# A convolution-and-MLP kernel on one core: halving the first chunk, doubling weights on ScalarE, softmax one chunk ahead, and the last addition by an accumulating DMA

## The chip, the cores and the metric

One core of a Trainium2 chip. The metric is the time on the device in microseconds (us), median of several executions. The kernel before took 477.84 us when it was first timed (477.68 to 479.58, 3 runs). All profiles used here are of undisturbed ("fast") executions; the profiler's span is some 1.5 us shorter than the time (476.3 against 477.84). "Clock" is the clock that TensorE was granted, as a share of its full one.

## The reference

For every position a softmax over 7 taps in each of 8 heads gives weights for a causal convolution of x. Its output goes through a layer that is the larger of two products, and through an output product.

```python
B, S, D, H, K = 8, 4160, 192, 8, 7           # F = 1024
w = np.exp(weight_gen - weight_gen.max(-1, keepdims=True))
w = w / (w.sum(-1, keepdims=True) + 1e-9)     # softmax over the K taps
x_pad = concat([zeros(B, K-1, D), x], axis=1)
y[b,s,h,:] = sum_k w[b,s,h,k] * x_pad[b, s+k, h,:]       # 24 values per head
g = np.maximum(y @ w1, y @ w2)                # 33280 x 1024
out = g @ w_out                               # 33280 x 192
```

## The kernel before

Each of 128 partitions holds 260 consecutive positions ("columns"). They are cut into chunks: three of 8 columns (0, 1, 2), fourteen of 16 (3 to 16), and two of 8 and 4. TensorE works in units of 8 columns (chunk 0 is two units of 4). The maximum is computed as y·w1 + relu(y·(w2−w1)); wd is w2−w1, and w10E, w10O, w10R are w1·w_out, computed on the chip at the start.

In these traces engines run their own instructions in program order, and so do the queues from which SyncE (SP) and GpSimd (POOL) issue DMAs: what the program writes earlier stands ahead.

```python
def conv(ci):                                   # VectorE, one chunk
    ...
    nc.vector.reduce_sum(out=sum_t, in_=...)    # e_t is exp(weight_gen), by ScalarE
    nc.vector.reciprocal(out=rec_t, in_=sum_t)
    nc.vector.tensor_tensor(                    # softmax product, each weight written twice
        out=_sub(en_t, 0, [[2, TH], [2 * TH, K], [1, 2]]),
        in0=_sub(e_t, 0, [[K, TH], [1, K], [0, 2]]),
        in1=_sub(rec_t, 0, [[1, TH], [0, K], [0, 2]]), op=ALU.mult)
    nc.vector.tensor_tensor(out=m_t, ...)       # weights times x, all taps ("product")
    if ci + 2 < len(CHUNKS):
        load(ci + 2)                            # POOL: wg_t and xb_t
    ... three additions: 7 taps to 1, the last into y_t
...
def transpose(u):                               # SP: y_t transposed into yt
    nc.sync.dma_start_transpose(out=yt..., in_=y_ts[ci]...)
def evac(u, i):                                 # ScalarE: 384 columns of TensorE's output to o_t
    nc.scalar.copy(...)
    ... after the last: nc.sync.dma_start(out=out..., in_=o_t)
...
for u in range(NU + 1):
    while queued < NCH and queued <= UNITS[min(u + 3, NU - 1)][0]:
        exp(queued); conv(queued); queued += 1
    if u == 0: transpose(0)
    if u + 1 < NU: transpose(u + 1)
    for i in range(4):                          # quarters of a unit on TensorE
        hid_main(u, 2 * i); hid_rest(u, 2 * i); relu(u, 2 * i) ...
        evac of the pair of columns before; output matmuls of unit u - 1; second hid, relu
```

The softmax here doesn't subtract the row's maximum and nothing guards it: scores larger than these inputs give would overflow.

## Time and profile before

| quantity | before | view it is read from |
|---|---|---|
| time | 477.84 us | times |
| span | 476.3 us | page |
| VectorE, one 16-column chunk | 25.61 us | timeline, from product to product |
| TensorE, one chunk at full clock | 25.24 us | timeline, eight quarters of 3.155 us |
| first hidden matmul / first of chunk 3 | 31.4 / 88.41 us | timeline |
| from chunk 3 to the end | 387.9 us | 476.3 − 88.41 |

The slices of the page (the span in 40 parts of 11.9 us; a digit is the busy share in tenths) for TensorE, VectorE and the granted clock:

```profile
PE   0087695599999999999999999989999999999997
DVE  2949999999999999999999999999999999997000
PEclk9999698599999999999999999999999999999999
```

From the ninth slice on (after 95 us), TensorE is full but for one slice at 8 and the end, and its clock is at 9 tenths or over.

In the group rows that follow, and in the prediction, a row gives line, engine, operation, output<-inputs, their shapes and the count, then busy us in all and mean ns of one, then idle us before them and what ended it. PE is TensorE, DVE VectorE, ACT ScalarE; PEld is the loading of weights, SPq SP's queue.

### The profile page before, as it was taken

The page shows a single profiled execution, that of the slowest core. Times are in us where ns is not written, and L with a number is a line of the kernel's source. Part 1 is how long each engine was busy: PE and PEld are TensorE (multiplying, and loading weights), DVE is VectorE, ACT ScalarE, POOL GpSimd, SP SyncE. Part 2 cuts the span into 40 slices and gives each one's busy share as a digit, 9 for nine tenths or more (in the row PEclk, how much of TensorE's full clock was granted, in tenths as well). Part 3 has the DMA queues.
Part 4 walks back from the last instruction along what each step waited for, and adds up shares of the span by engine and source line. Part 5 has one row for each costly group of instructions (what it writes and reads, how often), then busy time and mean ns, then how long its engine had stood idle before and what let it go on. Part 6 is the DMA issues. An engine that isn't in the chain of part 4 may idle for free.

```text
span 476.3 us, 8155 instructions
## 1 busy us (share of the span) xinstructions
PE 427.1 (90%) x3606; PEld 271.5 (57%) x3606; DVE 418.6 (88%) x136; ACT 336.5 (71%) x437; POOL 22.1 (5%) x46
## 2 busy tenths in 40 slices
PE   0087695599999999999999999989999999999997
PEld 0054353366666666666666666656666666666675
DVE  2949999999999999999999999999999999997000
ACT  1266374287877878787878787867878787777773
POOL 3000000000000000000000000000000000000000
PEclk9999698599999999999999999999999999999999
DMA  8945745546574737467585747384736537273212
GB/s 168 261 107 104 170 120 129 133 93 169 131 175 123 199 107 174 150 139 190 131 200 125 206 85 219 76 192 109 200 109 139 172 67 200 43 200 100 83 67 100
DMA packets 62131, 67.47 MB, mean 142 GB/s; under 512 B 52329, under 2 KB 53609, under 8 KB 60304
## 3 DMA queue, kind: packets, MB, share of 16 engines
q1 hardware_dynamic: 57792, 41.12, 31.1%
q0 software_dynamic: 4304, 25.84, 24.9%
q8 instruction: 28, 0.46, 0.4%
q14 instruction: 7, 0.06, 0.0%
HBM read 46.58 MB, written 25.56 MB: 151 GB/s over the span
## 4 chain that ended last, share of the span: by engine, by line
PE 81%; DVE 11%; DMA 5%; SPq 1%; ACT 1%; issue 0%; POOLq 0%
PE op_ps L292 34%; PE hdp L243 22%; PE hdp L258 13%; PE op_ps L279 7%; DVE m_t L138 5%; PE op_ps L287 4%; DMA wso<-in_moe_w_out_dram 3%; DVE m_t L149 2%; DMA yt<-y_t 2%; DVE m_t L151 1%; DVE en_t L130 1%; PE pw L211 1%; DVE y_t L154 1%; DMA wg_t<-in_weight_gen_dram 1%; DVE sum_t L125 1%; DVE rec_t L127 1%
## 5 line engine op out<-in xcount | busy, mean ns | idle before, releaser
L269 ACT ACTIVATE rd_t<-hdp 128x1024 bf16<-128x1024 f32 (+1 forms) x272 | 267.5, 986 | 112.0 <-PE hdp L258 77.2
L292 PE MATMUL op_ps<-wo,rd_t 128*128 128x192 bf16 x2080 | 216.6, 248 | 0.0
L292 PEld LDWEIGHTS <-rd_t 128*128 128x128 bf16 x2080 | 177.8, 99 | 23.7 <-issue 0.9
L138 DVE TENSOR_TENSOR m_t<-xb_t,en_t 128x21504 bf16<-128x21504 bf16 (+2 forms) x19 | 185.0, 9738 | 5.5 <-DMA xb_t<-zero_t 4.9
L243 PE MATMUL hdp<-yt,wdE 128*128 128x512 bf16 (+1 forms) x272 | 101.6, 374 | 20.8 <-DMA yt<-y_t 18.3
L243 PE MATMUL hdp<-yt,wdO 128*128 128x512 bf16 (+1 forms) x272 | 101.5, 373 | 0.0
L258 PE MATMUL hdp<-yt,wdR 64*128 64x512 bf16 (+1 forms) x544 | 81.6, 375 | 1.1 <-ACT rd_t L269 1.1
L149 DVE TENSOR_TENSOR m_t<-m_t 128x9216 bf16<-128x9216 bf16 (+2 forms) x19 | 81.0, 4263 | 0.7
L303 ACT COPY o_t<-op_ps 128x384 f32<-128x384 f32 x130 | 61.6, 474 | 2.5 <-PE op_ps L292 2.3
L151 DVE TENSOR_TENSOR m_t<-m_t 128x6144 bf16<-128x6144 bf16 (+2 forms) x19 | 55.0, 2894 | 0.7
L258 PEld LDWEIGHTS <-wdR 64*128 64x128 bf16 x544 | 16.2, 94 | 58.1 <-issue 57.5
L279 PE MATMUL op_ps<-w10R,yt 128*128 128x384 bf16 x130 | 44.0, 339 | 0.0
L279 PEld LDWEIGHTS <-yt 128*128 128x128 bf16 x130 | 12.4, 96 | 53.1 <-issue 52.8
L243 PEld LDWEIGHTS <-wdE 128*128 128x128 bf16 x272 | 26.8, 99 | 22.0 <-DMA yt<-y_t 19.6
L287 PEld LDWEIGHTS <-yt 128*128 128x128 bf16 x260 | 25.7, 99 | 14.8 <-issue 0.6
L130 DVE TENSOR_TENSOR en_t<-e_t,rec_t 128x1792 bf16<-128x1792 bf16 (+2 forms) x19 | 33.4, 1755 | 0.7
L287 PE MATMUL op_ps<-w10E,yt 128*128 128x192 bf16 x130 | 32.2, 248 | 0.0
L287 PE MATMUL op_ps<-w10O,yt 128*128 128x192 bf16 x130 | 32.2, 248 | 0.0
L154 DVE TENSOR_TENSOR y_t<-m_t 128x3072 bf16<-128x3072 bf16 (+2 forms) x19 | 29.0, 1527 | 0.7
L243 PEld LDWEIGHTS <-wdO 128*128 128x128 bf16 x272 | 26.8, 99 | 3.6 <-issue 3.4
L125 DVE TENSOR_REDUCE sum_t<-e_t 128x128 f32<-128x896 bf16 (+2 forms) x19 | 17.9, 944 | 9.9 <-ACT e_t L115 9.9
L105 POOL DMA_DIRECT2D xb_t<-in_x_dram x18 | 9.5, 529 | 333.4 <-DVE m_t L138 333.4
(29 smaller groups left out, 69.0 us busy)
## 6 DMA issues: line engine op xcount, KB each, us to landing
out_dram<-o_t SPq DMA_DIRECT2D x31, 768.0 KB, 3.9
xb_t<-in_x_dram POOLq DMA_DIRECT2D x14, 1056.0 KB, 7.8
wg_t<-in_weight_gen_dram POOLq DMA_DIRECT2D x14, 448.0 KB, 6.1
xb_t<-in_x_dram POOLq DMA_DIRECT2D x3, 672.0 KB, 7.9
wg_t<-in_weight_gen_dram POOLq DMA_DIRECT2D x4, 224.0 KB, 5.5
wso<-in_moe_w_out_dram SPq DMA_DIRECT2D x1, 768.0 KB, 13.5
out_dram<-o_t SPq DMA_DIRECT2D x2, 384.0 KB, 3.6
yt<-y_t SPq DMA_TRANSPOSE x34, 3.8
```

The source lines that it names most:

```text
L130: nc.vector.tensor_tensor(out=_sub(en_t, 0, [[2, TH], [2 * TH, K], [1, 2]]), in0=_sub(e_t, 0, [[K, TH], [1, K], [0, 2]]), in1=_sub(rec_t, ...
L138: nc.vector.tensor_tensor(out=m_t, in0=_sub(xb_t, 0, [[D, K], [1, n]]), in1=_sub(en_t, 0, [[2 * TH, K], [2, TH], [0, D // H // 2], [1, 2]] ...
L149: nc.vector.tensor_tensor(out=m_t[:, 0:3 * n], in0=m_t[:, 0:3 * n], in1=m_t[:, 3 * n:6 * n], op=ALU.add)
L151: nc.vector.tensor_tensor(out=rows(m_t, 2, 2, 0), in0=rows(m_t, 2, 2, 0), in1=rows(m_t, 5, 2, 1), op=ALU.add)
L154: nc.vector.tensor_tensor(out=y_t, in0=m_t[:, 0:n], in1=m_t[:, 2 * n:3 * n], op=ALU.add)
L243: nc.tensor.matmul(hd_ts[u, f][:, j * 512:j * 512 + N], lhsT=wd[kind][:, f * P:(f + 1) * P], rhs=_sub(yt_ts[u], 2 * j * P, [[3 * P, n // 2 ...
L258: nc.tensor.matmul(hd_ts[u, f][:, j * 512:j * 512 + N], lhsT=wd["R"][r, f * P:(f + 1) * P], rhs=_sub(yt_ts[u][r, :], P, [[3 * P, n // 2], ...
L269: nc.scalar.activation(out=_sub(rd_ts[u], f * 1024, [[512, 2], [1, N]]), in_=_sub(hd_ts.pop((u, f)), 0, [[512, 2], [1, N]]), func=AF.Relu,)
L279: nc.tensor.matmul(op[:, 0:2 * D], lhsT=yt[:, (3 * i + 1) * P:(3 * i + 2) * P], rhs=w10R, start=True, stop=False, skip_group_check=True,)
L287: nc.tensor.matmul(op[:, sl], lhsT=yt[:, (3 * i + 2 * j) * P:(3 * i + 2 * j + 1) * P], rhs=(w10E, w10O)[j], start=False, stop=False, skip_ ...
L292: nc.tensor.matmul(op[:, sl], lhsT=rd[:, f, j * 512 + i * P:j * 512 + (i + 1) * P], rhs=wo[:, f * D:(f + 1) * D], start=False, stop=(f == ...
L303: nc.scalar.copy(out=o_ts[u][:, 2 * i * D:2 * (i + 1) * D], in_=op_ts.pop((u, i))[:, 0:2 * D])
```

## The change

The intent is to take work off VectorE, the slower of two balanced engines, and to start earlier. The first chunk is computed in two halves, and its halo (the six positions ahead of it) is masked by a bitwise AND in place of a DMA of zeros. From chunk 2 on the softmax product writes each weight once, and ScalarE doubles it (dup). The softmax runs a chunk ahead. The last addition becomes an accumulating DMA. The weights' subtraction moves to GpSimd, and two evacuations become one of 768 columns. The transposes move to the end of the unit before. The functions are soft (the softmax), mul (the product), adds (the additions) and dup.

```diff
+            halo = xb_t[:, 0:PAD * D].bitcast(I32)
+            nc.vector.tensor_scalar(out=halo, in0=halo, scalar1=msk[:, 0:1], scalar2=None,
+                                    op0=ALU.bitwise_and)
...
-            out=_sub(en_t, 0, [[2, TH], [2 * TH, K], [1, 2]]),
+                out=_sub(en_t, 0, [[pair, N], [pair * N, K], [1, pair]]),   # pair is 1 from chunk 2
...
+    def dup(ci):
+        nc.scalar.copy(out=_sub(en_t, 0, [[2, KTH], [1, 2]]),
+                       in_=_sub(e1_ts.pop(ci), 0, [[1, KTH], [0, 2]]))
...
+            nc.vector.tensor_tensor(out=z_t, in0=m_t[:, 0:n], in1=m_t[:, n:2 * n], op=ALU.add)
+            nc.vector.tensor_tensor(out=y, in0=m_t[:, 2 * n:3 * n], in1=m_t[:, 6 * n:7 * n], op=ALU.add)
+            nc.gpsimd.dma_start(out=y, in_=z_t, accum_op=ALU.add, max_dma_last_dim=4096)
...
-            nc.vector.tensor_tensor(out=dst, in0=ws[kind, 1], in1=ws[kind, 0], op=ALU.subtract)
+            nc.gpsimd.tensor_tensor(out=dst, in0=ws[kind, 1], in1=ws[kind, 0], op=ALU.subtract)
+        soft(1)
+        mul(1)
+        load(3)
...
         nc.gpsimd.memset(w10R, 0.0)            # unchanged, but load(3) now stands ahead of it
...
-        if u + 1 < NU:
-            transpose(u + 1)
         for i in range(4):
...
+            if ca is not None:                 # u is the last unit of chunk ca - 1
+                if i == 1:
+                    dup(ca + 1); adds(ca); mul(ca + 1); load(ca + 3)
+                if i == 2:
+                    exp(ca + 2); soft(ca + 2)
+            if i == 3 and u + 1 < NU:
+                transpose(u + 1)
```

(The conditions for the last chunks left out.)

More of the change, by code (lines that the diff above doesn't have):

```diff
@@ L11 @@
 BF16 = mybir.dt.bfloat16
+I32 = mybir.dt.int32
 AF = mybir.ActivationFunctionType
@@ L41 @@
     FCH = F // P
+    DIRECT = 2
     CPP = B * S // P
@@ L76 @@
     wg_ts, xb_ts, y_ts, yt_ts = {}, {}, {}, {}
-    e_ts = {}
-    zero_t = consts.tile([P, PAD * D], BF16, name="zero_t")
-    nc.vector.memset(zero_t, 0.0)
+    e_ts, e1_ts, en_ts, m_ts = {}, {}, {}, {}
+    msk = consts.tile([P, 1], I32, name="msk")
+    nc.gpsimd.iota(msk, pattern=[[0, 1]], base=0, channel_multiplier=1)
+    nc.vector.tensor_single_scalar(out=msk, in_=msk, scalar=RPB - 1, op=ALU.bitwise_and)
+    nc.vector.tensor_scalar(out=msk, in0=msk, scalar1=1, scalar2=-1, op0=ALU.min, op1=ALU.mult)
     def load(ci):
@@ L84, in load @@
         wg_t = pwg.tile([P, To * WGC], FP32, name="wg_t", tag="wg")
-        nc.gpsimd.dma_start(
+        (nc.sync if ci == 0 else nc.gpsimd).dma_start(
             out=wg_t,
@@ L92, in load @@
         if c0 == 0:
+            nc.gpsimd.memset(xb_t[0:1, 0:PAD * D], 0.0)
             nc.gpsimd.dma_start(
@@ L102, in load @@
             )
-            nc.sync.dma_start(out=xb_t[0:P:RPB, 0:PAD * D], in_=zero_t[0:P:RPB, :])
+            halo = xb_t[:, 0:PAD * D].bitcast(I32)
+            nc.vector.tensor_scalar(out=halo, in0=halo, scalar1=msk[:, 0:1], scalar2=None,
+                                    op0=ALU.bitwise_and)
         else:
@@ L116, in exp, with pieces, soft @@
         e_ts[ci] = e_t
-    def conv(ci):
-        To = sum(CHUNKS[ci][1])
-        n = To * D
-        TH = To * H
+    def pieces(ci):
+        return [(0, 4), (4, 4)] if ci == 0 else [(0, sum(CHUNKS[ci][1]))]
+    def soft(ci):
+        TH = sum(CHUNKS[ci][1]) * H
         e_t = e_ts.pop(ci)
@@ L127, in conv @@
         nc.vector.reciprocal(out=rec_t, in_=sum_t)
-        en_t = pen.tile([P, K * TH * 2], BF16, name="en_t", tag="en")
+        pair = 2 if ci < DIRECT else 1
+        for o, To in pieces(ci):
+            N = To * H
+            if pair == 2:
+                en_t = pen.tile([P, K * N * 2], BF16, name="en_t", tag=f"en{o}")
+                en_ts[ci, o] = en_t
+            else:
+                en_t = pe_.tile([P, K * N], BF16, name="e1_t", tag="e1")
+                e1_ts[ci] = en_t
+            nc.vector.tensor_tensor(
+                out=_sub(en_t, 0, [[pair, N], [pair * N, K], [1, pair]]),
+                in0=_sub(e_t, o * WGC, [[K, N], [1, K], [0, pair]]),
+                in1=_sub(rec_t, o * H, [[1, N], [0, K], [0, pair]]),
+                op=ALU.mult,
+            )
@@ new lines, in dup, with mul @@
+    def dup(ci):
+        if ci not in e1_ts:
+            return
+        KTH = K * sum(CHUNKS[ci][1]) * H
+        en_t = pen.tile([P, KTH * 2], BF16, name="en_t", tag="en0")
+        nc.scalar.copy(out=_sub(en_t, 0, [[2, KTH], [1, 2]]),
+                       in_=_sub(e1_ts.pop(ci), 0, [[1, KTH], [0, 2]]))
+        en_ts[ci, 0] = en_t
+    def mul(ci, o=0):
+        To = dict(pieces(ci))[o]
+        n = To * D
+        m_t = pm.tile([P, K * n], BF16, name="m_t", tag="m")
+        m_ts[ci, o] = m_t
@@ L130, in conv @@
         nc.vector.tensor_tensor(
-            out=_sub(en_t, 0, [[2, TH], [2 * TH, K], [1, 2]]),
-            in0=_sub(e_t, 0, [[K, TH], [1, K], [0, 2]]),
-            in1=_sub(rec_t, 0, [[1, TH], [0, K], [0, 2]]),
+            out=m_t,
+            in0=_sub(xb_ts[ci], o * D, [[D, K], [1, n]]),
+            in1=_sub(en_ts[ci, o], 0, [[2, K * To * H], [0, D // H // 2], [1, 2]]),
             op=ALU.mult,
         )
-        xb_t = xb_ts.pop(ci)
-        m_t = pm.tile([P, K * n], BF16, name="m_t", tag="m")
@@ L138, in conv, with adds, rows @@
-        nc.vector.tensor_tensor(
-            out=m_t,
-            in0=_sub(xb_t, 0, [[D, K], [1, n]]),
-            in1=_sub(en_t, 0, [[2 * TH, K], [2, TH], [0, D // H // 2], [1, 2]]),
-            op=ALU.mult,
-        )
-        if ci + 2 < len(CHUNKS):
-            load(ci + 2)
-        def rows(t, step, cnt, at):
-            return _sub(t, at * n, [[step * n, cnt], [1, n]])
+    def adds(ci, o=0):
+        T_all = sum(CHUNKS[ci][1])
+        n = dict(pieces(ci))[o] * D
+        m_t = m_ts.pop((ci, o))
+        def rows(at, step, cnt):
+            return _sub(m_t, at * n, [[step * n, cnt], [1, n]])
@@ L149, in conv @@
         nc.vector.tensor_tensor(out=m_t[:, 0:3 * n], in0=m_t[:, 0:3 * n],
                                 in1=m_t[:, 3 * n:6 * n], op=ALU.add)
-        nc.vector.tensor_tensor(out=rows(m_t, 2, 2, 0), in0=rows(m_t, 2, 2, 0),
-                                in1=rows(m_t, 5, 2, 1), op=ALU.add)
-        y_t = py.tile([P, n], BF16, name="y_t", tag="y")
-        nc.vector.tensor_tensor(out=y_t, in0=m_t[:, 0:n], in1=m_t[:, 2 * n:3 * n], op=ALU.add)
-        y_ts[ci] = y_t
+        if o == 0:
+            y_ts[ci] = py.tile([P, T_all * D], BF16, name="y_t", tag="y")
@@ new lines, in adds @@
+        y = y_ts[ci][:, o * D:o * D + n]
+        if ci < DIRECT:
+            nc.vector.tensor_tensor(out=rows(0, 2, 2), in0=rows(0, 2, 2), in1=rows(1, 5, 2),
+                                    op=ALU.add)
+            nc.vector.tensor_tensor(out=y, in0=m_t[:, 0:n], in1=m_t[:, 2 * n:3 * n], op=ALU.add)
+        else:
+            z_t = py.tile([P, n], BF16, name="z_t", tag="z")
+            nc.vector.tensor_tensor(out=z_t, in0=m_t[:, 0:n], in1=m_t[:, n:2 * n], op=ALU.add)
+            nc.vector.tensor_tensor(out=y, in0=m_t[:, 2 * n:3 * n], in1=m_t[:, 6 * n:7 * n],
+                                    op=ALU.add)
+            nc.gpsimd.dma_start(out=y, in_=z_t, accum_op=ALU.add, max_dma_last_dim=4096)
@@ L159 @@
     load(0)
+    exp(0)
+    soft(0)
     ident = consts.tile([P, P], BF16, name="ident")
@@ L183 @@
         )
-        exp(0)
-        conv(0)
+        exp(1)
+        for o in (0, 4):
+            mul(0, o)
+            adds(0, o)
+        load(2)
         for kind, dst in (("E", wd["E"]), ("T", wd["R"][0:64, :])):
-            nc.vector.tensor_tensor(out=dst, in0=ws[kind, 1], in1=ws[kind, 0], op=ALU.subtract)
+            nc.gpsimd.tensor_tensor(out=dst, in0=ws[kind, 1], in1=ws[kind, 0], op=ALU.subtract)
+        soft(1)
+        mul(1)
+        load(3)
         nc.sync.dma_start(out=wd["R"][64:P, :], in_=wd["E"][0:64, :])
@@ L276, in out_first @@
         yt = yt_ts[u]
-        op = pps_o.tile([P, 512], FP32, name="op_ps", tag="op")
-        op_ts[u, i] = op
+        if i % 2 == 0:
+            op_ts[u, i // 2] = pps_o.tile([P, 1024], FP32, name="op_ps", tag="op")
+        op = op_ts[u, i // 2][:, i % 2 * 512:i % 2 * 512 + 2 * D]
         nc.tensor.matmul(
-            op[:, 0:2 * D], lhsT=yt[:, (3 * i + 1) * P:(3 * i + 2) * P], rhs=w10R,
+            op, lhsT=yt[:, (3 * i + 1) * P:(3 * i + 2) * P], rhs=w10R,
             start=True, stop=False, skip_group_check=True,
@@ L284, in out_col @@
     def out_col(u, i, j):
-        yt, rd, op = yt_ts[u], rd_ts[u], op_ts[u, i]
-        sl = slice(j * D, (j + 1) * D)
+        yt, rd, op = yt_ts[u], rd_ts[u], op_ts[u, i // 2]
+        sl = slice(i % 2 * 512 + j * D, i % 2 * 512 + (j + 1) * D)
         nc.tensor.matmul(
@@ L297, in out_col, with evac @@
             )
-    def evac(u, i):
+    def evac(u, g):
         ci, o, n = UNITS[u]
-        if i == 0:
+        if g == 0:
             o_ts[u] = pout.tile([P, n * D], FP32, name="o_t", tag="o")
-        nc.scalar.copy(out=o_ts[u][:, 2 * i * D:2 * (i + 1) * D],
-                       in_=op_ts.pop((u, i))[:, 0:2 * D])
-        last = u == NU - 1
-        if i == n // 2 - 1 or last:
-            a = 2 * i if last else 0
-            b = 2 * i + 2
+        nc.scalar.copy(out=_sub(o_ts[u], 4 * g * D, [[2 * D, 2], [1, 2 * D]]),
+                       in_=_sub(op_ts.pop((u, g)), 0, [[512, 2], [1, 2 * D]]))
+        if g == n // 4 - 1:
             nc.sync.dma_start(
-                out=bass.AP(tensor=out.tensor, offset=(CHUNKS[ci][0] + o + a) * D,
-                            ap=[[CPP * D, P], [1, (b - a) * D]]),
-                in_=o_ts[u][:, a * D:b * D],
+                out=bass.AP(tensor=out.tensor, offset=(CHUNKS[ci][0] + o) * D,
+                            ap=[[CPP * D, P], [1, n * D]]),
+                in_=o_ts[u],
             )
     NCH = len(CHUNKS)
-    queued = 1
+    exp(2)
+    soft(2)
+    transpose(0)
     prev_evac = None
     for u in range(NU + 1):
-        while queued < NCH and queued <= UNITS[min(u + 3, NU - 1)][0]:
-            exp(queued)
-            conv(queued)
-            queued += 1
-        if u == 0:
-            transpose(0)
-        if u + 1 < NU:
-            transpose(u + 1)
+        ends_chunk = u < NU - 1 and UNITS[u + 1][0] != UNITS[u][0]
+        ca = UNITS[u][0] + 1 if ends_chunk else None
         for i in range(4):
@@ L349 @@
                 out_col(u - 1, q, 1)
-                prev_evac = (u - 1, q)
+                if q % 2 == 1:
+                    prev_evac = (u - 1, q // 2)
+            if ca is not None:
+                if i == 1:
+                    if ca + 1 < NCH:
+                        dup(ca + 1)
+                    adds(ca)
+                    if ca + 1 < NCH:
+                        mul(ca + 1)
+                    if ca + 3 < NCH:
+                        load(ca + 3)
+                if i == 2 and ca + 2 < NCH:
+                    exp(ca + 2)
+                    soft(ca + 2)
+            if i == 3 and u + 1 < NU:
+                transpose(u + 1)
     if prev_evac is not None:
```

## The prediction

> **What bounds the kernel now.** I read the page's header and slices first, then the groups by line and shape, then busy time by stretch, then the timeline in order of time at the places where TensorE stands still. The group rows that carry the steady state:
>
> ```profile
> PE 427.1 (90%) x3606; PEld 271.5 (57%) x3606; DVE 418.6 (88%) x136; ACT 336.5 (71%) x437; POOL 22.1 (5%) x46
> ...
> L138 DVE TENSOR_TENSOR m_t<-xb_t,en_t 128x21504 bf16<-128x21504 bf16 x14 | 159.0, 11359 | 0.5
> L149 DVE TENSOR_TENSOR m_t<-m_t 128x9216 bf16<-128x9216 bf16 x14 | 69.4, 4958 | 0.5
> L303 ACT COPY o_t<-op_ps 128x384 f32<-128x384 f32 x130 | 61.6, 474 | 2.5 <-PE op_ps L292 2.3
> L151 DVE TENSOR_TENSOR m_t<-m_t 128x6144 bf16<-128x6144 bf16 x14 | 47.0, 3357 | 0.5
> L130 DVE TENSOR_TENSOR en_t<-e_t,rec_t 128x1792 bf16<-128x1792 bf16 x14 | 28.4, 2025 | 0.5
> L154 DVE TENSOR_TENSOR y_t<-m_t 128x3072 bf16<-128x3072 bf16 x14 | 24.6, 1758 | 0.5
> L125 DVE TENSOR_REDUCE sum_t<-e_t 128x128 f32<-128x896 bf16 x14 | 15.1, 1078 | 0.0
> L127 DVE RECIPROCAL rec_t<-sum_t 128x128 f32<-128x128 f32 x14 | 13.3, 953 | 0.5
> ```
>
> There are 14 full chunks of 16 columns. VectorE's seven rows sum to 11.36+4.96+3.36+2.03+1.76+1.08+0.95 = 25.5 us; in the timeline its products start 25.61 us apart. TensorE repeats a quarter of an 8-column unit every 3.155 us, so a chunk costs it 8 x 3.155 = 25.24 us. The two engines are balanced to 1.5%, VectorE being the slower. Busy time by stretch shows where this balance is not yet reached:
>
> ```profile
> 40.00:50.00 10.00, 4.31 (x41) 2.63 (x37) 9.79 (x8) 4.02 (x8) 1.07 (x2) 0.83 0.87 187
> 80.00:90.00 10.00, 1.59 (x6) 0.27 (x6) 9.86 (x6) 0.00 (x0) 0.00 (x0) 0.54 0.68 155
> 200.00:300.00 100.00, 100.00 (x859) 63.69 (x856) 99.17 (x29) 79.70 (x100) 4.28 (x8) 1.00 0.63 157
> ```
>
> (Columns: stretch, length, busy PE, PEld, DVE, ACT, POOL, then granted clock, DMA share, GB/s.) Until 90 us TensorE starves while VectorE is full; afterwards both are full. The timeline ties them:
>
> ```profile
> 82.76 1.76 DVE L154 TENSOR_TENSOR y_t<-m_t 128x3072 bf16<-128x3072 bf16 x1
> ...
> 313.28 1.76 DVE L154 TENSOR_TENSOR y_t<-m_t 128x3072 bf16<-128x3072 bf16 x1
> ...
> 320.38 0.39 PE L243 MATMUL hdp<-yt,wdE 128*128 128x512 bf16 x1 [1.76 <-DMA yt<-y_t]
> ```
>
> Chunk 3 (counting from 0), the first full one, leaves VectorE at 84.5, its transpose lands, and TensorE resumes at 88.41 (3.9 us later). At 320 TensorE has used up its lead and waits again. So **the end is set by "when does y leave VectorE, plus its way to TensorE"**, not by busy shares.
>
> [...] the 1056 KB x load, which reads twice that in fp32, took 7.8 us to land, [...] exp over 448 and 896 elements took 570 and 943 ns, slope 0.833. [...]
>
> **The change part by part.**
>
> *VectorE, full chunk.* The weights are no longer written twice: 896 instead of 1792 elements, 1.09 us (the measured 128x896 form) for 2.03, saves 0.93. The adds of 3.36+1.76 become two of 3072 elements, 2 x 1.76, saves 1.6. VectorE needs 25.5-2.5 = 23.0 us. It stops being the bound.
>
> *ScalarE, full chunk.* The doubling copy of 1792 elements costs 0.19+0.833 x 1792 = 1.69 us. Two 384-column evacuations of 0.474 become one 768-column one, about 0.8 by the slope, four times: saves 0.6. Its load goes from 20.1 us (measured in 25.24) to about 21.2, still under 25.24. But ScalarE works in program order, and the doubling, an evacuation and the exp fall within one and a half quarters of a unit. From the steady timeline: relu of an odd tile ends 3.63 us after its quarter begins and its buffer is needed again at 3.95, a slack of 0.3. After the doubling, the fifth tile's relu waits for relu, 1.59 doubling, 0.92 relu, 0.70 evacuation (durations less about 0.1 overlap) and ends 4.66 into the next quarter instead of 3.63, 0.7 past need. So **TensorE loses about 0.7 us per chunk**, 25.24 to 25.9.
>
> *The new loop.* The order of instructions shows: in the last unit of chunk c, VectorE does adds(c+1), product(c+2), softmax(c+3); product(c+2) needs the doubling, which ScalarE does only after the fourth relu of that unit. With c starting on TensorE at 0: last unit at 12.6; fourth relu starts 5.8 later, 0.9, doubling 1.7: 21.1. Product 11.4, softmax of the next chunk 3.1, adds 8.5: y(c+2) leaves VectorE at 44.1. Then the accumulating DMA, new on the path: [...] 5.6 us, call it an estimate. Then the transpose 3.9. **Chunk c+2 can start at 53.7, where TensorE wants it at 2 x 25.24 = 50.5 (51.9 with the doubling's stalls).**
>
> *Start.* The zero-row DMA goes (VectorE waited 4.9 us for it), and the weight loads start some 5 us earlier. But x and weights then share the DMA rates, so I start the first product at 12 as before, at best 9.5. The subtraction on GpSimd stands behind the load of chunk 2, which waits for the second half's product: about 21 us, done by 25 to 27, hence first matmul near 31 as before. VectorE's work to y(3): 11.7 (two halves) +2.3+5.8+1.8+5.3+5.8+3.1+4.5+11.4+3.1+8.5 = 63.2 us (the 1.8 being softmax(2)), plus 1.7 waiting for the doubling of chunk 2: 77. Plus 5.6+3.9: TensorE starts chunk 3 at 86, against 88.4. The missing idle of 6.6 us (waiting for an exp at 32 us) is mostly paid back by the DMA add.
>
> *Sum.* Chunk 3 at 86; chunk 4 at 86+25.9 = 111.9; then two chunks per 53.7: chunk 16 at 111.9+6 x 53.7 = 434.1. From chunk 16's start (421.35) to the span's end was 55.0 before; with the stall 55.7. Span 489.8, plus 1.5 between span and time: **491 us**.
>
> **Rivals.**
> A. *The DMA add is quick (below 4 us).* For: DMA is idle then, since the x load was issued when the product ended. Then TensorE bounds with doubling stalls: 86+13 x 25.9+55.7+1.5 = 480.
> B. *Neither costs anything*, the intended outcome: 86+13 x 25.24+55+1.5 = 470.6, 1.5% faster. More than 2% needs chunk 3 to start below 83.7 and no loss later: possible only if x lands at 9.5.
> C. *Long stalls cool the clock.* Before, stalls of 6 to 10 us were followed by matmuls at half speed; the 1.76 us stall at 320 was not. My stalls are 2 to 3 us. If they cool it, about 1.7 us is added at each of six: 501. The same end follows if the add takes 7.5 us.
> D. *GpSimd's subtraction and VectorE block each other* at 21 to 28 us: up to 4 us later at the start, largely hidden.
>
> **Range and chances.** Main line 491, A 480, B 471, C 501. Weighted mostly on main line and A I say 489, range 474 to 502. The 2% lines are 468.3 and 487.4: faster 0.09, within 0.33, slower 0.58.
>
> **What would show it.** The DMA add's issue to landing near 5.6 us; TensorE waiting on the transpose about 3 us at every second chunk, the chain of waits running through product, adds, DMA add and transpose; VectorE idle before products, waiting for the doubling copy, and busy 23.0 per chunk; short waits of TensorE for relu after each doubling; chunk 3 starting near 86. I am wrong if the add takes under 4 us, if the doubling runs earlier than 21 us into the chunk, or if the first y comes much before 20 us.

## More of the kernel before

SP's own waits (what ended the wait: total us, times, longest):

```profile
SPq L227 <- DVE y_t L154: 271.5, 17, 19.1
```

SP mostly stands ready at a transpose and waits for y_t, so a transpose is issued as soon as VectorE is done. How long the transposes then take, from the view of the tile yt:

```profile
DMA to landing us min/median/max: 2.9/3.8/5.5
```

None takes over 5.5 us; this is to be held against the same line of later kernels.

## The result

The changed kernel takes 553.64 us (median, 552.77 to 554.76, 4 runs) against 477.76 for the kernel before in the same rounds. The ratio is 1.158, with a 95% interval of 1.154 to 1.162: **slower by 15.8%**. Ratios here are the mean time of one kernel's runs over that of the other's of the same rounds, all of them fast but for two of x1's, so they are not quite the ratio of the medians. The direction was predicted; the size, 489 in a range of 474 to 502, was not.

The page of the changed kernel: busy times, then slices of TensorE and of the clock.

```profile
PE 445.6 (81%) x3606; PEld 277.7 (50%) x3606; DVE 424.7 (77%) x141; ACT 351.8 (64%) x389; POOL 49.1 (9%) x66
...
PE   0518756399969999699959997799959995999996
...
PEclk9959779599998999799988999799979999899999
```

TensorE has the same 3606 matmuls but 18.5 us more busy time, and every fourth or fifth slice is a hole in PE and in its clock. VectorE, meant to be relieved, is busy 424.7 us instead of 418.6. The groups by shape and the DMA issues (KB each, median us from issue to landing) say why:

```profile
L147 DVE TENSOR_TENSOR e_t<-e_t,rec_t 128x896 bf16<-128x896 bf16 x14 | 58.1, 4151 | 0.5
...
L160 ACT COPY en_t<-e_t 128x1792 bf16<-128x1792 bf16 x14 | 23.5, 1678 | 0.5 <-DVE e_t L147 0.5
```

```profile
y_t<-z_t POOLq DMA_DIRECT2D x14, 768.0 KB, 7.2
```

The softmax product, half the elements, takes 4.15 us where it took 2.03. The doubling copy costs 1.68 us, as predicted (1.69). The DMA add takes 7.2 us. The waits (total, times, longest):

```profile
DVE m_t L170 <- ACT en_t L160: 80.7, 16, 13.0
...
PE hdp L295 <- DMA yt<-y_t: 60.3, 10, 12.6
...
PE hdp L295 <- ACT w10R L268: 11.9, 1, 11.9
```

VectorE stands before its products for 80.7 us in all, waiting for the doubling (the longest, 13.0, before the last chunk of 4 columns). TensorE waits 60.3 us for transposes and 11.9 us for w10R. One round of the loop, from the timeline (start, duration, engine, line, operation; in brackets the idle time before and what ended it):

```profile
166.62 0.61 PE L295 MATMUL hdp<-yt,wdE 128*128 128x512 bf16 x1 [5.92 <-DMA yt<-y_t]
...
187.30 1.68 ACT L160 COPY en_t<-e_t 128x1792 bf16<-128x1792 bf16 x1
...
189.01 11.36 DVE L170 TENSOR_TENSOR m_t<-xb_t,en_t 128x21504 bf16<-128x21504 bf16 x1 [7.67 <-ACT en_t L160]
...
202.38 4.14 DVE L147 TENSOR_TENSOR e_t<-e_t,rec_t 128x896 bf16<-128x896 bf16 x1
...
213.02 1.75 DVE L197 TENSOR_TENSOR y_t<-m_t 128x3072 bf16<-128x3072 bf16 x1
...
215.08 1.23 POOL L199 DMA_DIRECT2D y_t<-z_t  x1 [13.87 <-DVE y_t L197]
...
222.37 1.42 SPq L279 DMA_TRANSPOSE yt<-y_t  x1
...
226.06 0.61 PE L295 MATMUL hdp<-yt,wdE 128*128 128x512 bf16 x1 [5.92 <-DMA yt<-y_t]
```

This is a closed chain: the doubling stands behind ScalarE's fourth relu, which waits for TensorE; it lets VectorE multiply, and two steps later TensorE gets its input, two chunks further on. It takes 59.4 us here, and 60.3 on average over six rounds ((467.67 − 105.86)/6, the starts of chunks 3 and 15), where TensorE's work needs 50.5.

The start, in the timelines of GpSimd (its subtractions, load(3) and the memset), VectorE (the second half's last two additions) and TensorE (the first hidden matmul):

```profile
23.37 2.76 POOL L236 TENSOR_TENSOR wdE<-ws1E,ws0E 128x1024 bf16<-128x1024 f32 x1
26.09 3.04 POOL L236 TENSOR_TENSOR wdR<-ws1T,ws0T 64x1024 bf16<-64x1024 f32 x1
...
37.88 0.54 POOL L114 DMA_DIRECT2D xb_t<-in_x_dram  x1 [8.23 <-DVE m_t L170]
38.42 0.43 POOL L258 MEMSET w10R<- 128x384 bf16 x1
```

```profile
23.96 2.98 DVE L191 TENSOR_TENSOR m_t<-m_t 128x1536 bf16<-128x1536 bf16 x1
26.98 2.58 DVE L193 TENSOR_TENSOR y_t<-m_t 128x768 bf16<-128x768 bf16 x1
```

```profile
39.59 0.37 PE L295 MATMUL hdp<-yt,wdE 128*128 128x256 bf16 x1 [11.95 <-ACT w10R L268]
```

The first half's same additions took 0.96 and 0.56 us, so VectorE lost 4.0 us beside the subtraction. That the subtraction is the cause is shown by the later runs that have it on VectorE, as x8:

```profile
24.57 0.96 DVE L199 TENSOR_TENSOR m_t<-m_t 128x1536 bf16<-128x1536 bf16 x1
25.56 0.56 DVE L201 TENSOR_TENSOR y_t<-m_t 128x768 bf16<-128x768 bf16 x1
```

The small memset of w10R (0.43 us) stands in GpSimd's queue behind load(3), which waited 8.23 us for chunk 1's product. So w10R came late and the first hidden matmul came at 39.6 instead of 31.4. Chunk 3 starts at 105.86 instead of 88.41.

### The profile page after: what moved, and what is told of

It reads as the page before. It is cut to its first block, busy times and chain, and to the rows that moved or that the text cites. A ratio compares the mean times of both kernels' runs of the same rounds, so it can differ in the third digit from the quotient of the medians.

```text
span 551.4 us, 8159 instructions
## 1 busy us (share of the span) xinstructions
PE 445.6 (81%) x3606; PEld 277.7 (50%) x3606; DVE 424.7 (77%) x141; ACT 351.8 (64%) x389; POOL 49.1 (9%) x66
## 4 chain that ended last, share of the span: by engine, by line
issue 64%; PE 18%; DVE 7%; DMA 6%; POOL 4%; ACT 1%; POOLq 0%; DVEq 0%; SPq 0%; ACTq 0%
PE op_ps L345 8%; PE hdp L295 5%; DVE m_t L170 4%; PE hdp L310 3%; DMA y_t<-z_t 3%; POOL wg_t L91 2%; DMA xb_t<-in_x_dram 2%; PE op_ps L332 2%; DMA yt<-y_t 1%; POOL y_t L199 1%; PE op_ps L340 1%; DVE m_t L191 1%; DVE y_t L193 1%; DVE m_t L185 0%; POOL xb_t L114 0%
## 5 line engine op out<-in xcount | busy, mean ns | idle before, releaser
L170 DVE TENSOR_TENSOR m_t<-xb_t,en_t 128x21504 bf16<-128x21504 bf16 (+2 forms) x20 | 185.2, 9258 | 80.9 <-ACT en_t L160 80.7
L345 PE MATMUL op_ps<-wo,rd_t 128*128 128x192 bf16 x2080 | 220.8, 251 | 0.0
L345 PEld LDWEIGHTS <-rd_t 128*128 128x128 bf16 x2080 | 181.6, 100 | 25.8 <-issue 3.1
L295 PE MATMUL hdp<-yt,wdE 128*128 128x512 bf16 (+1 forms) x272 | 104.7, 385 | 73.5 <-DMA yt<-y_t 60.3
L295 PE MATMUL hdp<-yt,wdO 128*128 128x512 bf16 (+1 forms) x272 | 104.9, 386 | 0.0
L310 PE MATMUL hdp<-yt,wdR 64*128 64x512 bf16 (+1 forms) x544 | 87.3, 390 | 7.6 <-ACT rd_t L321 7.6
L185 DVE TENSOR_TENSOR m_t<-m_t 128x9216 bf16<-128x9216 bf16 (+2 forms) x20 | 84.7, 4234 | 0.1
L147 DVE TENSOR_TENSOR e_t<-e_t,rec_t 128x896 bf16<-128x896 bf16 (+2 forms) x17 | 63.6, 3740 | 0.6
L357 ACT COPY o_t<-op_ps 128x768 f32<-128x768 f32 x65 | 51.7, 795 | 2.7 <-PE op_ps L345 2.5
L199 POOL DMA_DIRECT2D y_t<-z_t x17 | 19.9, 1169 | 240.6 <-DVE y_t L197 240.6
L196 DVE TENSOR_TENSOR z_t<-m_t 128x3072 bf16<-128x3072 bf16 (+2 forms) x17 | 27.1, 1593 | 0.6
```

The costliest lines, as they stand in the source:

```text
L147: nc.vector.tensor_tensor(out=_sub(en_t, 0, [[pair, N], [pair * N, K], [1, pair]]), in0=_sub(e_t, o * WGC, [[K, N], [1, K], [0, pair]]), i ...
L170: nc.vector.tensor_tensor(out=m_t, in0=_sub(xb_ts[ci], o * D, [[D, K], [1, n]]), in1=_sub(en_ts[ci, o], 0, [[2, K * To * H], [0, D // H // ...
L185: nc.vector.tensor_tensor(out=m_t[:, 0:3 * n], in0=m_t[:, 0:3 * n], in1=m_t[:, 3 * n:6 * n], op=ALU.add)
L196: nc.vector.tensor_tensor(out=z_t, in0=m_t[:, 0:n], in1=m_t[:, n:2 * n], op=ALU.add)
L295: nc.tensor.matmul(hd_ts[u, f][:, j * 512:j * 512 + N], lhsT=wd[kind][:, f * P:(f + 1) * P], rhs=_sub(yt_ts[u], 2 * j * P, [[3 * P, n // 2 ...
L310: nc.tensor.matmul(hd_ts[u, f][:, j * 512:j * 512 + N], lhsT=wd["R"][r, f * P:(f + 1) * P], rhs=_sub(yt_ts[u][r, :], P, [[3 * P, n // 2], ...
```

## The experiments

Four suspects: the layout of the softmax product, the place of the doubling, the DMA add, and the order in the queues at the start. The rival to all of them is that parts of the same chain hide each other, so that undoing one gains little. "Edit" is against the changed kernel unless said otherwise. All results were correct, except where said. Overview:

| run | what | us | over before (95%) |
|---|---|---|---|
| changed kernel | | 553.64 | 1.158 (1.154 to 1.162) |
| x1_layout | contiguous softmax product | 534.13 | 1.119 (1.110 to 1.127) |
| x2_vector_add | no DMA add | 515.48 | 1.080 (1.076 to 1.084) |
| x3_memset_early | memset ahead of the loads | 548.06 | 1.148 (1.144 to 1.151) |
| x4_dup_early | doubling 6 to 9 us earlier | 510.45 | 1.068 (1.064 to 1.072) |
| x5_plain_copy | DMA copies, does not add (wrong) | 533.98 | 1.118 (1.112 to 1.124) |
| x6_layout_dup_early | x1 and x4 | 503.03 | 1.053 (1.050 to 1.057) |
| x7_vector_all | doubling and addition on VectorE | 495.72 | 1.038 (1.034 to 1.042) |
| x8_combined | x6, x2, x3, subtraction on VectorE | 497.53 | 1.040 (1.035 to 1.045) |
| x9_transpose_early | transposes ahead in SP's queue | 552.01 | 1.158 (1.155 to 1.162) |
| x10_combined_transpose | x8 and x9 | 485.60 | 1.018 (1.015 to 1.021) |
| x11_vector_all_transpose | x7, x9, x3, subtraction | 477.83 | 1.003 (1.000 to 1.005) |
| x12_before_transpose_late | kernel before, transposes late | 478.46 | 1.004 (1.000 to 1.007) |
| x13_split_doubling | x10, doubling in three pieces | 476.96 | 0.997 (0.994 to 1.000) |
| x14_vector_all_late | x11 without x9 | 478.22 | 1.000 (0.997 to 1.003) |
| x15_split_dma_add | x13 with the DMA add | 479.70 | 1.003 (1.000 to 1.006) |

### One part at a time: x1 to x5

x1_layout: VectorE writes contiguously, ScalarE puts in order while doubling (shortened here).

```diff
-                out=_sub(en_t, 0, [[pair, N], [pair * N, K], [1, pair]]),
+                out=_sub(e1_t, 0, [[K, N], [1, K]]),
...
-        nc.scalar.copy(out=_sub(en_t, 0, [[2, KTH], [1, 2]]), in_=_sub(e1, 0, [[1, KTH], [0, 2]]))
+        nc.scalar.copy(out=_sub(en_t, 0, [[2*N, K], [2, N], [1, 2]]), in_=_sub(e1, 0, [[1, K], [K, N], [0, 2]]))
```

> One edit on the changed kernel: VectorE writes the single weights in the order in which it reads them (contiguous), and ScalarE reorders while it doubles. Theory S (the softmax product costs 4.15 us because each bf16 result goes alone to a place 256 bytes from the last): it falls to about 1.1 us, the way from the doubling to y falls by 3.1, two chunks take 55 to 56 us instead of 60.4, chunk 3 starts some 7 us earlier, total 510 to 520 us. Rival (the 4.15 us come from another engine's use of memory, or from reading one element at a time): it stays above 3.5 us and the total near 553. If ScalarE's doubling gets slower by writing far apart (over 2.5 us for 1.68), the gain is partly lost in the stall of TensorE after it.

Its groups by shape:

```profile
L168 ACT COPY en_t<-e_t 128x1792 bf16<-128x1792 bf16 x14 | 24.6, 1760 | 0.0
...
L147 DVE TENSOR_TENSOR e_t<-e_t,rec_t 128x896 bf16<-128x896 bf16 x14 | 15.3, 1092 | 0.5
```

Same inputs and count, contiguous output: 1.09 instead of 4.15 us, and ScalarE pays 0.08 us for the ordering. The output's layout alone is the cause. The median fell by 19.5 us only, and it mixes two fast runs (527.5 and 531.4) with two slow (536.9 and 539.8). By the fast runs the gain is 22 to 26 us, still short of the 510 to 520 expected, and chunk 3 started 2.9 us earlier (103.0), not 7. The chain still begins with the doubling: VectorE's wait for it grew from 80.7 to 100.5 us. In the profiled run two chunks take 56.5 us ((443.2 − 160.8)/5).

x2_vector_add: the last addition stays on VectorE (`if ci < DIRECT:` becomes `if True:`).

> One edit on the changed kernel: the last addition back on VectorE (3.36 + 1.76 us for 2 x 1.76), no accumulating DMA. Theory A (the 7.2 us of the DMA add lie on the chain that releases TensorE): the chain for two chunks falls by about 6 us to 53-54, but VectorE then has 27.8 us of work per chunk and becomes the bound at 55.6 us for two; total 512 to 522 us, TensorE waits on the transpose still[...]. Rival (the DMA add is hidden and VectorE's work alone counts): total 553 or above, up to 575.

515.5 us, as expected. Per round the DMA's 7.2 us go from the chain and 1.6 us of VectorE come back (3.36 + 1.76 for twice 1.76). Of the gain of 38 us, 5.5 come at the start (chunk 3 at 100.36); the 32.7 after it are near six times the difference (34). Chunks now take 27.65 us, which is VectorE's own work, as the theory had it; most stalls are 1 to 3 us, and the mean clock rises from 0.926 to 0.971.

x3_memset_early: `nc.gpsimd.memset(w10R, 0.0)` moved ahead of load(2).

> One edit on the changed kernel: the zeroing of the last weight tile goes ahead of the loads of chunks 2 and 3 on GpSimd's queue. Theory Q (it stood behind a load that waits for the product of chunk 1, and held the first matmul until 39.6 us): first matmul at 31 to 33 us; VectorE's wait of 2.6 us for the exp of chunk 2 goes; chunk 3 starts 3 to 5 us earlier because VectorE's work bounds the start, total 548 to 551 us. Rival (the whole 8 us go through to the end): 545. Second rival (nothing of it reaches the end): 553.

548.1 us, as expected, with chunk 3 at 101.2, 4.7 us earlier. The first hidden matmul is at 34.86, not at 31 to 33: it now waits 5.94 us for its transpose.

x4_dup_early: in the full chunks dup(ca + 1) moves from the second quarter of a chunk's last unit to the end of its first unit.

```diff
-                    if ca + 1 < NCH:
-                        dup(ca + 1)
...
+            if (i == 3 and ca is None):        # first unit of a full chunk
+                dup(UNITS[u][0] + 2)
```

> One edit on the changed kernel: for full chunks ScalarE doubles the weights at the end of the first unit of the chunk two before, some 6 to 9 us earlier. Theory G (the product waits for the doubling, which TensorE's own progress releases, and this closes a loop of 60 us for two chunks): VectorE's idle time ahead of the products (80 us in sum) falls below 20, VectorE becomes the bound with 26.2 us per chunk, total 500 to 510 us. Rival (the loop is closed by DMA add and transpose, not by the doubling): VectorE waits elsewhere, total above 540.

510.5 us: just over the 500 to 510 expected. VectorE's wait for the doubling falls from 80.7 us, though not below 20:

```profile
DVE m_t L170 <- ACT en_t L160: 27.8, 16, 9.8
```

This is the largest gain among x1 to x5, 43 us, though the 4.15 us product and the DMA add are still there. VectorE, with 26.2 us of work a chunk, is then nearly the bound: chunks take 26.5 us ((427.9 − 163.1)/10 in the profiled run).

x5_plain_copy (relative error 0.58): the DMA overwrites instead of adding. Its output is wrong, which doesn't matter for the time.

```diff
-            nc.gpsimd.dma_start(out=y, in_=z_t, accum_op=ALU.add, max_dma_last_dim=4096)
+            nc.gpsimd.dma_start(out=y, in_=z_t, max_dma_last_dim=4096)
```

> Wrong result on purpose: the accumulating DMA of the changed kernel becomes a plain DMA of the same bytes on the same queue, so that y is overwritten instead of added to. Theory R [...]: issue to landing falls from 7.2 us to about 4 us, the chain for two chunks from 60.4 to 55-57, total 515 to 532 us. Rival (the 7.2 us come from the queue and from the load of the next weights that is issued 0.7 us behind it): it stays above 6 us and the total above 545.

```profile
y_t<-z_t POOLq DMA_DIRECT2D x14, 768.0 KB, 4.2
```

The transfer takes 4.2 instead of 7.2 us: the adding is 3.0 us of it. What in the adding takes them, this run can't tell. The time is 534.0 (two runs), 2 us over the range expected. Of the gain of 19.7 us, 3.9 come before chunk 3 (102.0) and 13.8 after it in the profiled run, where six rounds by 3.0 would be 18.

### Together: x6 to x8

x6_layout_dup_early is x1 and x4 together.

> The changed kernel with two edits together: contiguous weights on VectorE, and ScalarE's doubling at the end of the first unit of a full chunk. The DMA add stays. Theory (VectorE 23.1 us per chunk, chain for two chunks about 46 us, under the 50.5 of TensorE): TensorE never waits for a transpose by more than 1 us after chunk 3, which still starts at 103, so total 488 to 497 us; what is left above the kernel before is the late start. Rival (the DMA add stays on the path by itself): waits on the transpose in every second chunk, total above 503.

503.0, 6 us over the range: the two together gain 50.6 us where they gained 22 to 26 and 43.2 alone, for they cut the same chain. The start was hardly touched: chunk 3 at 102.8. The rival's number was met, but not in its way: no stall on a transpose in the loop is over 1.4 us, and chunks take 26.1 to 26.8 us, mostly for a reason that x13 shows.

x7_vector_all: `DIRECT = 2` becomes `DIRECT = 99`, so every chunk has VectorE's paired product and its last addition, as before.

> The changed kernel with VectorE writing the doubled weights itself and doing the last addition for all chunks (no ScalarE doubling, no DMA add); halves, mask, softmax one chunk ahead, GpSimd subtraction and paired evacuation stay. Theory (the loss of the steady state comes from those two parts alone): VectorE 25.6 us per chunk as before, no idle after chunk 3, which starts at 92, total 479 to 484 us; the 2 to 6 us above the kernel before come from the start. Rival (paired evacuation or the order of the softmax also cost): above 490.

495.7, a miss of 12 us. Both new parts of the loop are undone, but TensorE starts chunk 3 at 102.4. x8_combined takes x6 and x2 with the start mended (memset early, subtraction on VectorE).

> All mends together: contiguous weights, early doubling, last addition on VectorE, the zeroing ahead of the loads on GpSimd, the subtraction back on VectorE. Expected: first matmul at 31 to 33 us, chunk 3 at 84 to 88, VectorE 24.6 us per chunk and TensorE the bound at 25.24 plus 0.3 to 0.6 of waits for ScalarE after each doubling: total 471 to 477 us, 0 to 1.4% faster than the kernel before. Rival (ScalarE's doubling costs TensorE more than VectorE gains): 478 to 485.

497.5, a miss of 20 us. There the start is nearly mended (chunk 3 at 90.2, not 84 to 88), but the loop is not: chunk 3 to the end takes 402.1 us (before 387.9). So two different things were left. I suspected the one part not yet touched: the change writes transpose(u + 1) at the end of a unit, behind the output DMA in SP's queue. SP's waits in x8:

```profile
SPq L368 <- ACT o_t L365: 322.0, 34, 16.2
```

SP now waits for evacuations, not for y_t.

### The transposes' place: x9 to x12 and x14

x9_transpose_early moves only this:

```diff
+        if ca is not None:
+            adds(ca)
+        if u + 1 < NU:
+            transpose(u + 1)
         for i in range(4):
...
-                    adds(ca)
...
-            if i == 3 and u + 1 < NU:
-                transpose(u + 1)
```

> The changed kernel with one thing moved: in the program each unit's transposing DMA (and the adds it depends on) is written at the start of the unit before, as in the kernel before, instead of at its end, so that it stands in SP's queue ahead of the output DMA of two units earlier. Order on VectorE, ScalarE, TensorE and GpSimd stays. Theory: at the start TensorE's two stalls near 59 and 78 us shrink from about 6 us to under 3, but chunk 3 and the loop are set by VectorE's 4.15 us softmax product and by the DMA add, so every second chunk still takes about 60 us and most of the gain is given back: 543 to 552 us (after: 553.6). Rival: the transposes' place was the main loss all along; then 500 to 520 us.

552.0, at the upper end of the theory's range: nothing gained. The loop's stalls of 5.9 us stay, since there y_t itself is late. At the start the theory held by half: the first of the two stalls fell from 5.6 to 0.4 us, the second grew from 6.0 to 8.2. x10_combined_transpose is x8 with this move:

> The combined repair (contiguous softmax product on VectorE with ScalarE ordering and doubling it, doubling early, last addition on VectorE, memset and subtraction as before; 497.5 us) with the transposing DMAs moved ahead as well. Theory: its remaining 20 us over the kernel before are the transposes that wait in SP's queue behind an output DMA that in turn waits for the paired evacuation (322 us of SP's waiting in that run), then start together with the loads and land 13 us later. With them ahead the queue waits for y_t instead, the stalls of 3.4 and 2.4 us in every two chunks go, and the time is 467 to 477 us, at or under the kernel before. Rival: the transposes are slow because they collide with the loads, wherever they stand; then the stalls stay and it is over 488 us.

485.6, 12 us less than x8 but 9 over the range. x11_vector_all_transpose is x7 with this move and the start mended:

> The changed kernel with its first chunk in halves and its mask kept, but softmax product paired on VectorE for all chunks, no ScalarE doubling, last addition on VectorE, memset and subtraction as before, and the transposing DMAs ahead. VectorE's work per chunk is then that of the kernel before (25.6 us). Theory: 472 to 481 us, the same as before within 2%. Rival (the order of softmax one chunk ahead or the paired evacuation itself costs the rest): about 488 to 496 us, as without the move (495.7).

477.8, level with before. So the halves of the first chunk, the mask, softmax ahead and the paired evacuation together neither gain nor cost over 0.5%. x12_before_transpose_late does the opposite, in the kernel before:

```diff
-        if u + 1 < NU:
-            transpose(u + 1)
         for i in range(4):
...
+            if i == 3 and u + 1 < NU:
+                transpose(u + 1)
```

> The kernel before with one part of the change alone: each transposing DMA is written at the end of the unit before instead of at its start. Theory: SP then waits for the evacuation and no longer for y_t, each transpose is issued about a quarter into the unit before, some 9 us ahead of its use, and lands late where it meets loads: 484 to 496 us against 477.6. Rival: 9 us are enough for a transpose of 4 us where nothing else was changed, and the place in the queue costs only in company with the other parts: 476 to 481 us.

478.5: the rival was right. x14_vector_all_late, x11 without the move, parts the two edits between x7 and x11:

> As x11 (all work on VectorE, memset and subtraction mended, 477.8 us), but the transposes late, as in the changed kernel. Theory: at the start y_t is ready with little to spare, each late transpose adds some 4 to 6 us to units 1 and 2 and chunk 3 starts near 92 us instead of 87.7; in the loop the rest of x7's drift (some 4 us) stays: 483 to 489 us. Rival: the memset and subtraction were all of it (the loop has slack for a late transpose, as in the kernel before with late transposes): 477 to 480 us.

478.2: again the rival. **My theory of the transposes fell in this general form**: the mended start was all of x7's loss, and the late place costs nothing clear of noise in x12 and x14, yet some 12 us in x8 (in the profiled runs of x8 and x10, 4.3 before chunk 3 and 5.8 after it). The traces show a difference. Time to landing in x8, then in x14:

```profile
DMA to landing us min/median/max: 3.1/5.1/12.9
```

```profile
DMA to landing us min/median/max: 3.3/4.6/6.5
```

In x8's loop a transpose and the loads of x are issued in the same moment (147.15 and 147.45 us), it lands 12.9 us later and TensorE waits 3.39 us; in x14 the transpose goes at 245.18 and the load at 248.74, 3.6 us later. In x7's start they meet too (54.63 and 55.49): that transpose takes 10.7 us to land, so the late w10R's 7.7 us (first hidden matmul at 40.4 against 32.7 in x14) grow to 14.5 at chunk 3 (102.4 against 87.9). That the meeting with the loads is the cause is read from these traces. No run moved the loads alone, so it stays argued.

### What was left: x13 and x15

x10's loop has no wait of TensorE over 0.7 us after 100 us, yet its chunks take 26.1 us. ScalarE (start, duration) and TensorE in its timeline:

```profile
231.60 1.75 ACT L168 COPY en_t<-e_t 128x1792 bf16<-128x1792 bf16 x1
233.25 1.03 ACT L329 ACTIVATE rd_t<-hdp 128x1024 bf16<-128x1024 f32 x1
234.16 0.80 ACT L365 COPY o_t<-op_ps 128x768 f32<-128x768 f32 x1
234.84 1.97 ACT L329 ACTIVATE rd_t<-hdp 128x1024 bf16<-128x1024 f32 x2
```

```profile
235.95 0.39 PE L318 MATMUL hdp<-yt,wdR 64*128 64x512 bf16 x2 [0.66 <-ACT rd_t L329]
```

The doubling, a relu, an evacuation and a relu stand back to back, and TensorE waits 0.66 us for the last. This is the stall that the prediction worked out as 0.7 us. x13_split_doubling cuts the doubling into pieces of 2, 2 and 3 taps, one in each of the second, third and fourth quarters of the chunk's first unit (the edit is against x10; the last piece starts 13.0 us into the chunk, as the whole did):

```diff
-                    else (i == 3 and ca is None)):
-                dup(UNITS[u][0] + 2)
+                elif ca is None and i > 0:
+                    dup(UNITS[u][0] + 2, ((0, 2), (2, 4), (4, K))[i - 1])
```

> The combined repair with early transposes (485.6 us), with ScalarE's doubling cut into three pieces (2, 2 and 3 taps) that stand between relus instead of one piece of 1.75 us. Theory: the one piece delays a relu, TensorE waits 0.66 us and its second unit of every chunk takes 13.5 us instead of 12.65; 15 chunks by 0.85 is 12 us. In pieces the stall goes: 472 to 477 us, a chunk in 25.3 us. Rival: ScalarE is simply too full for the doubling (81% busy), three pieces stall TensorE three times: 484 to 488 us.

476.96, 0.3% under the kernel before in the same rounds (interval 0.994 to 1.000), which counts as the same. The timeline shows no wait of TensorE after 110 us, and a chunk takes 25.24 us. The pieces take 0.64, 0.64 and 0.86 us, 0.4 more in sum than one piece, and that is harmless. No run put one whole piece earlier, so the pieces are shown to be enough, not to be needed. x15_split_dma_add keeps the DMA add as well, so it has all parts of the change, in a mended order, but for the subtraction on GpSimd:

> As x13 with the accumulating DMA for the last addition kept: all three ideas of the change are in it, only their order and the layout of the softmax product are mended. Theory: y_t is ready over 15 us ahead of its transpose's use in the loop, so 7 us more are hidden, and at the start chunks 2 and 3 come some 2 to 4 us later: 474 to 481 us, within 1% of x13. Rival: [...] SP's queue stands behind it: 485 us or more.

479.7. Chunk 3 starts at 90.9 (x13: 87.4), and from there to the end takes 385.5 us (x13: 387.7). The DMA add is hidden in the loop, where y_t is early, and costs 3.5 us at the start, where y_t is awaited; 2.7 us of that are left in the time.

## Why the prediction was wrong

**The bound before: right.** The end is set by y's way to TensorE, and both engines are balanced. What I did not draw from it: at full clock TensorE needs 25.24 us a chunk whatever the change does. Before, x13 and x14 take 387.9, 387.7 and 388.7 us from chunk 3 to the end (x15 385.5). Little but the start could pay.

**VectorE's chunk: wrong, the failed step.** "896 instead of 1792 elements, 1.09 us (the measured 128x896 form) for 2.03". The row of that size before wrote pairs: 4 bytes together at each place. The new one writes single 2-byte values 256 bytes apart, and took 4.15 us; written contiguously it took 1.09 (x1), so 3.4 ns less for each of the 896 values. So VectorE's chunk became 26.2 us (11.36 + 1.08 + 0.95 + 4.15 + 5.16 + 1.76 + 1.75), not 23.0. "It stops being the bound" was false: that is more than TensorE's 25.24, and x4 came to 26.5 a chunk. In the changed kernel itself neither engine but the chain below was the bound, at 30.15 us a chunk, and the slow product stands in it. The saving in the additions, 1.6 us, was real.

**The accumulating DMA: place right, size off.** It was on the path, as predicted. The 5.6 us were my estimate, with no accumulating DMA in the trace before to read it from; measured were 7.2 for 768 KB (4.1 for 384 KB). x5 showed that the adding costs 3.0 of the 7.2 (4.2 us as a plain copy).

**The loop's chain: right in shape, mis-sized.** The predicted steps sum to 53.7 us, the measured round to 59.4. The end of the doubling came at 22.4 us instead of 21.1 (+1.3, behind a first quarter at a low clock); product, softmax and additions took 25.8 instead of 23.0 (+2.8); from y_t to the transpose 7.6 instead of 5.6 (+2.0); the transpose 3.7 instead of 3.9 (−0.2). The sum is +5.9, and the two rounds differ by 5.7; the rest is rounding. Six rounds at their mean of 60.3 are 40 us more than six of 53.7.

**Rival C: happened, beyond its size.** "My stalls are 2 to 3 us" became 5.9 us, each of which halved the clock (0.50 to 0.52 in the 3.1 us after each of the six): the first quarter after 226.06 took 5.5 us instead of 3.155, 2.3 us more (1.3 to 2.7 in the six; the rival's 1.7 was my estimate). In x1 the loop has nine stalls of 1.07 to 2.99 us. After eight of them the first matmul (512 columns) took 0.39 us; after the one of 2.44 us it took 0.61, as after the 5.9 us. After x8's stall of 3.39 us it took 0.39, so the length of a stall alone does not decide. The rival named the effect; the chain's other errors brought it on.

**The start: wrong.** "Hence first matmul near 31" came at 39.6. I counted GpSimd's subtraction but not the memset behind load(3) in its queue. Chunk 3 was predicted at 86 and came at 105.9. I trace the 20 us as: first product 1.6 us later (its x landed at 13.24 us beside the weights, before at 9.22); rival D's 4.0, which was not "largely hidden" since VectorE was the bound there; 2.6 waiting for an exp that stood behind the late w10R; the three softmax products 1.5 + 3.1 + 3.1; waits for the doubling some 2; the DMA add 1.6. Sum 19.5; the prediction's own terms give 86.5, not 86. Of these x3 confirms 4.7 by experiment, and runs with the subtraction on VectorE lose the 4.0. In the trace the subtractions started first, and VectorE's additions, 0.96 and 0.56 us alone, took 2.98 and 2.58 us and ended 0.8 and 0.4 us after them.

**The doubling's stall of TensorE: right** (0.7 predicted; 0.66 in x10, where a chunk takes 26.07 us against the 25.9 predicted). In the changed kernel it occurs 13 times (7.6 us in all), under the larger stalls.

**Sum:** 19.9 us at the start, 40 in the loop, 2 at the end make the 62 us between the 489.8 us of span predicted and the 551.4 measured. By these sums the slow softmax product alone is some 25 of them, as an estimate (six rounds by 2.8 and 7.7 at the start), and x1's fast runs gained 22 to 26. x15 keeps the ideas of the change but for the subtraction on GpSimd, in another order and layout, and is 74 us faster than the changed kernel.

## What to carry to other kernels

When an operation is made smaller, take its duration from a row with the same write pattern, not just the same element count (896 elements took 4.15 us here in one pattern, 1.09 in another), and test the layout alone before moving work around it. When work is handed from engine to engine, write down the closed chain with the queue that each step stands in: the same doubling and the same DMA add were links of a chain that lost 40 us in one order of the program, and cost nothing, or 3 us at the start, in another. Ask for each small instruction left in place what now stands ahead of it in its queue.
